# First two units of the Mlp on the attention's list, four weight blocks split in place, another list and another order of evictions

## Chip, cores and metric

The kernel runs on one core of one Trainium2 chip. The metric is the device time of one execution in microseconds, the median of several runs.

## What is computed

The kernel computes a delta-rule attention over 32 heads, then a first Mlp with a rational function between its two products, then a second one with mish.

```python
k_n = k / (np.linalg.norm(k, axis=-1, keepdims=True) + 1e-06)
for t in range(S):                     # q, k, v: (4, 8, 768, 48)
    y[:, :, t] = np.einsum('bhd,bhde->bhe', q[:, :, t], state)
    v_old = np.einsum('bhde,bhd->bhe', state, kt)
    state = state + bt[:, :, :, None] * np.einsum('bhd,bhe->bhde', kt, vt - v_old)
...
h = x @ w_in                           # x: (3072, 384), w_in: (384, 2048)
P = a[0] + a[1] * h + a[2] * h2 + a[3] * h3
Q = 1.0 + np.abs(b[0]) * np.abs(h) + np.abs(b[1]) * h2
x = (P / (Q + 1e-06)) @ w_out          # w_out: (2048, 384)
...
h = x @ w_in                           # the second Mlp, weights of its own
g = h * np.tanh(np.where(h > 20.0, h, np.log1p(np.exp(np.minimum(h, 20.0)))))
out = g @ w_out
```

The weights arrive as float64 and are turned into float32 on the chip.

## The kernel before

**Attention.** The 768 positions are twelve units u of 64, each holding 32 heads. `prepare` loads k and q of a unit, scales k by its norm (`kn`), transposes k and q on TensorE (PE) into `kq`, multiplies them (`gram`, L417) and writes the masked products on VectorE (DVE) into `gm` and `lg` (L426). For every pair of units `inverse` solves a triangular system in 30 steps of two operations (L501, L507), between an opening transpose on DVE (`first`, L489) that needs the masks of both units, and a closing one (`last`, L514) that gives `xt`. For u = 1 and 9 these steps run on DVE, for u = 3, 5, 7 and 11 on GpSimd (POOL). `step` then takes the units one after the other through the state: PE products with S (L561), with xt (L578), with gm (L593), the new state (L601), and y (L616), with small DVE and ScalarE (ACT) operations between them. Step u needs the state that step u-1 left and xt of its pair; xt of u=11 (`xt_152`) serves steps 10 and 11.

**Weights.** `Weights.convert` handles one side (w_in or w_out) of one f block of 128 of the 2048 columns: load the raw block, ACT takes the magnitude (`mag`, L717), DVE makes the float32 word in four operations in the PSUM bank `word` (L722 to L738), ACT writes the high part (`out`, L745) and POOL the rest (`rest`, L750). With high and low parts three matmuls stand for one exact product. Blocks 0 and 1 (`FQ`) stay in SBUF; blocks 2 to 15 are stored to memory and fetched again by the Mlp part.

**The list.** `Plan` holds each operation of the attention, of the first Mlp's weights and of x of the first group, with an engine, a guessed duration, what it reads and what it writes. `order` walks a model of the engines and takes, of what is ready, the operation with the longest tail, shifted by a bias out of the table `ORDER` (by engine, tile name and twelfth of the list). The cost formulas, `Clock` and `ORDER` thus decide the fixed order in which every engine runs. Where the model sees PE idle, matmuls of zeros (L1099) are put in.

**Mlp.** Each Mlp has 96 units: six groups of 512 tokens times sixteen f blocks. A unit is an "up" (nine 128x512 matmuls into one of two PSUM banks h, L870), elementwise work, and a "down" (L956, nine 128x512 matmuls into three of four banks o, or L989 in the second Mlp, twelve 128x384). `MLP_OPS` lists for one iteration, as two-letter operations, what is issued in which order; `LAGS` puts the down four units behind the up. For the first Mlp 1a to 1c are three ACT operations out of h (L900 to L909), 1d a POOL product (L913), 1e and 1f Ln and Exp on ACT (L920, L922) into one of two PSUM banks r, 1g and 1h two DVE operations that read h (L927, L929) and free its bank, 1i to 1k three DVE operations (L936 to L945) that give g; then g is split into a high part (L881) and a low part (L885). At the end of a group y0, y1 and y2 are the copies of the three o banks to SBUF (ACT, L1078); the next group's first down waits for them. In the first iterations only ups are there, so units 0 to 4 go up ahead of the first down. Five fetched blocks (`LOOK`) are asked for at the start of this part.

```python
"fx fw y0 1e 1f y1 u0 u1 u2 1a 1b 1c 1i 1j 1k 1d 1g 1h y2 d0 d1 d2 d3 xa 1L 1m xB f c",
w1.plan(plan, [*range(FQ, NF), *range(FQ)])
fetch_w = {n: (w1.fetch_split, FQ + LOOK + n) for n in range(NF - FQ - LOOK)}
```

Of the kernel before, what the change touches and what calls it, by code (L numbers as in the profile page):

```python
# [43 lines left out]
class Ring:  # L44
# [27 lines left out]
    'ACT s_ps': {-1: -732309, 0: 55802},  # L72
    'ACT w': {-1: 9850, 9: 213571, 10: -105072, 11: 10115},
    'ACT wm': {-1: -117229, 9: -1472, 10: 21445, 11: -42477},
    'ACT x': {-1: 910575, 11: 50160},
    'ACT yst': {-1: 297892, 2: 1553, 3: -60918, 4: 1728, 5: 12465, 6: 156789, 7: -104482, 8: -41027, 9: 6271},
# [30 lines left out]
class Clock:  # L107


    STEP, DOWN, UP, SMALL = 3413.0, 0.57, 0.85, 0.45  # L110

    def __init__(self):
        self.used = {i: self.STEP for i in range(-1, 4)}
        self.at, self.rate = 0, 1.0
# [1107 lines left out]
```

## Time and profile before

| what | us |
|---|---|
| median of three runs | 1132.39 |
| lowest and highest | 1126.92, 1140.34 |
| the profiled execution | 1140.86 |
| its span | 1138.4 |
| PE busy in the span | 1068.5 (94%) |
| first product h of the first Mlp | 322.19 |

The profile is one execution, recorded on the chip. "Busy" is the time in which an engine runs instructions; PE's granted clock is given as a share of its full speed. Idle time is put down to what came last. An "up" of unit i is written u*i*, a "down" d*i* where a list of matmuls is meant.

### The profile page before, as it was taken

The page shows a single profiled execution, that of the slowest core. Times are in us where ns is not written, and L with a number is a line of the kernel's source. Part 1 is how long each engine was busy: PE and PEld are TensorE (multiplying, and loading weights), DVE is VectorE, ACT ScalarE, POOL GpSimd, SP SyncE. Part 2 cuts the span into 40 slices and gives each one's busy share as a digit, 9 for nine tenths or more (in the row PEclk, how much of TensorE's full clock was granted, in tenths as well). Part 3 has the DMA queues.
Part 4 walks back from the last instruction along what each step waited for, and adds up shares of the span by engine and source line. Part 5 has one row for each costly group of instructions (what it writes and reads, how often), then busy time and mean ns, then how long its engine had stood idle before and what let it go on. Part 6 is the DMA issues. An engine that isn't in the chain of part 4 may idle for free.

```text
span 1138.4 us, 24584 instructions
## 1 busy us (share of the span) xinstructions
PE 1068.5 (94%) x10130; PEld 930.9 (82%) x10130; DVE 718.4 (63%) x1207; ACT 612.9 (54%) x1101; POOL 538.9 (47%) x622
## 2 busy tenths in 40 slices
PE   6787889788989999999999999999999999999998
PEld 6677778678867778788787878899999999999997
DVE  4987585896558999999999999994121111212110
ACT  4524445323458888888888888743333223333322
POOL 4187698675436777777777777764000000000000
PEclk8988698977799999999999999999999999999999
DMA  7437686415466031121203026160101001010000
GB/s 127 87 80 187 189 207 185 124 45 157 140 246 241 15 111 43 42 83 43 84 28 112 14 91 254 58 195 14 56 1 56 1 1 56 1 56 1 29 1 28
DMA packets 121263, 99.20 MB, mean 87 GB/s; under 512 B 79808, under 2 KB 104512, under 8 KB 121152
## 3 DMA queue, kind: packets, MB, share of 16 engines
q1 hardware_dynamic: 120896, 97.54, 28.5%
q8 instruction: 79, 1.29, 0.5%
q14 instruction: 32, 0.26, 0.1%
q0 software_dynamic: 256, 0.10, 0.1%
HBM read 66.16 MB, written 31.46 MB: 86 GB/s over the span
## 4 chain that ended last, share of the span: by engine, by line
PE 51%; POOL 15%; ACT 12%; DVE 10%; issue 7%; DMA 2%; SPq 2%; POOLq 0%; DVEq 0%; ACTq 0%
PE h L870 20%; PE o L989 18%; POOL q L913 8%; POOL gh L885 3%; POOL r L903 3%; ACT r L920 3%; PE y_ps L616 3%; PE o L956 3%; PE c_ps L578 2%; ACT q L900 2%; ACT r L922 2%; DVE tmp L501 2%; SPq L291 1%; PE s_all L601 1%; DVE gm L426 1%
## 5 line engine op out<-in xcount | busy, mean ns | idle before, releaser
L870 PE MATMUL h<-x,w 128*128 128x512 f32 x1728 | 430.2, 393 | 5.7 <-DMA w<-w 3.5
L870 PEld LDWEIGHTS h<-x,w 128*128 128x128 f32 x1728 | 322.2, 188 | 75.1 <-DVE s L929 7.2
L885 DVE TENSOR_TENSOR gh<-g,gh 128x512 fp32r<-128x512 f32 x80 | 55.4, 692 | 282.7 <-ACT g L980 282.7
L956 PE MATMUL o<-gh,w 128*128 128x512 f32 x864 | 213.4, 390 | 4.9 <-ACT ev L1078 4.9
L989 PE MATMUL o<-w,gh 128*128 128x384 f32 x1152 | 216.8, 337 | 0.0
L989 PEld LDWEIGHTS o<-w,gh 128*128 128x128 f32 x1152 | 204.6, 188 | 8.1
L956 PEld LDWEIGHTS o<-gh,w 128*128 128x128 f32 x864 | 161.6, 188 | 41.1 <-ACT ev L1078 7.8
L975 ACT ACTIVATE gh<-h 128x512 fp32r<-128x512 f32 x96 | 57.5, 599 | 235.8 <-PE h L870 235.7
L913 POOL TENSOR_TENSOR q<-q,r 128x512 f32<-128x512 f32 x96 | 124.5, 1297 | 71.1 <-ACT r L907 66.6
L885 POOL TENSOR_TENSOR gh<-g,gh 128x512 fp32r<-128x512 f32 x112 | 145.4, 1299 | 23.9 <-ACT g L980 21.4
L920 ACT ACTIVATE r<-q,cst 128x512 f32<-128x512 f32 x96 | 66.4, 692 | 52.6 <-POOL q L913 52.6
L936 DVE SCALAR_TENSOR_TENSOR q<-q,r 128x512 f32<-128x512 f32 x96 | 65.2, 679 | 15.1 <-ACT r L922 14.8
L909 ACT ACTIVATE s<-h,ab 128x512 f32<-128x512 f32 x96 | 74.3, 774 | 0.0
L929 DVE SCALAR_TENSOR_TENSOR s<-s,ab,h 128x512 f32<-128x512 f32 x96 | 71.8, 748 | 3.4
L750 POOL TENSOR_TENSOR w<-wm,w 128x384 fp32r<-128x384 f32 x48 | 49.8, 1040 | 48.6 <-ACT w L745 48.4
L940 DVE SCALAR_TENSOR_TENSOR r<-s,ab,r 128x512 f32<-128x512 f32 x96 | 71.6, 746 | 0.0
L927 DVE TENSOR_TENSOR s<-s,h 128x512 f32<-128x512 f32 x96 | 65.3, 681 | 9.5 <-ACT s L909 9.5
L945 DVE SCALAR_TENSOR_TENSOR g<-q,r 128x512 f32<-128x512 f32 x96 | 65.9, 687 | 3.3
L507 POOL TENSOR_TENSOR xs<-xs,tmp 128x30 f32<-128x30 f32 (+14 forms) x120 | 62.4, 520 | 9.4
L501 POOL TENSOR_TENSOR tmp<-xs 128x30 f32<-128x30 f32 (+14 forms) x120 | 59.4, 495 | 7.1
L881 ACT CAST gh<-g 128x512 fp32r<-128x512 f32 x96 | 59.7, 622 | 0.0
L903 POOL TENSOR_SCALAR r<-q,ab 128x512 f32<-128x512 f32 x54 | 42.1, 780 | 34.8 <-ACT q L900 34.8
(125 smaller groups left out, 1396.9 us busy)
## 6 DMA issues: line engine op xcount, KB each, us to landing
w<-w SPq DMA_DIRECT2D x36, 768.0 KB, 7.1
w<-in_moe_w_in_dram SPq DMA_DIRECT2D x32, 384.0 KB, 3.9
...
```

What stands on the lines that cost most here:

```text
L501: eng.tensor_tensor(out=tv, in0=ls[:, j, j + 1:HC].unsqueeze(1).to_broadcast([128, j, n]), in1=xs[:, 0:j, j:j + 1].to_broadcast([128, j, n ...
L870: self.nc.tensor.matmul(out=self.st[i]["h"], lhsT=self.w.t[f][:, a, 0, k], rhs=self.x[g][:, b, k], start=(n == 0), stop=(n == 8),)
L885: (nc.gpsimd if engine == "P" else nc.vector).tensor_tensor(out=s["gh"][:, 1], in0=s["g"], in1=s["gh"][:, 0].bitcast(F32), op=ALU.subtract)
L903: nc.gpsimd.tensor_scalar(out=s["r"], in0=s["q"], scalar1=k["b1"], scalar2=k["b0"], op0=ALU.mult, op1=ALU.add)
L909: nc.scalar.activation(out=s["s"], in_=s["h"], func=ACTF.Identity, scale=k["a3"], bias=k["a2"])
L913: nc.gpsimd.tensor_tensor(out=s["q"], in0=s["q"], in1=s["r"], op=ALU.mult)
L920: nc.scalar.activation(out=s["r"], in_=s["q"], func=ACTF.Ln, bias=k["c"])
L929: nc.vector.scalar_tensor_tensor(out=s["s"], in0=s["s"], scalar=k["a1"], in1=s["h"], op0=ALU.add, op1=ALU.mult)
L940: nc.vector.scalar_tensor_tensor(out=s["r"], in0=s["s"], scalar=k["a0"], in1=s["r"], op0=ALU.add, op1=ALU.mult)
L945: nc.vector.scalar_tensor_tensor(out=s["g"], in0=s["q"], scalar=2.0, in1=s["r"], op0=ALU.subtract, op1=ALU.mult, reverse0=True)
L956: self.nc.tensor.matmul(out=self.acc[g][d], lhsT=self.w.t[f][:, a, 1, d], rhs=self.st[i]["gh"][:, b], start=(first and n == 0), stop=(last ...
L989: self.nc.tensor.matmul(out=self.acc[g][t][:, 0:384], lhsT=self.st[i]["gh"][:, a, t * 128:(t + 1) * 128], rhs=self.w.t[f][:, b, 1].rearran ...
```

## The change

Six things are changed together.

- Four tiles `wg` of the size of a split weight block are allocated in the outer pool. While the attention runs they hold `gm` 0 to 3; once a gm is dead, one of the blocks 2 to 5 (`FG`) is split into it in place and stays there. Blocks 6 to 15 come first in the list and are the only ones that are stored and fetched again.
- Two tiles `gh` hold the attention's `qn`, and later the split g of units 0 and 1 (`FIRST`).
- The front of units 0 and 1 (up, elementwise work, split of g) joins the attention's list (`Mlp1.plan`). The up goes into the attention's banks `t_ps`; q, s, r and g lie in the buffers of kn 0 to 3, r in SBUF instead of a PSUM bank. The Mlp part leaves these steps out and runs the downs of units 0 and 1 in iterations 2 and 3.
- In the first Mlp's list the second eviction y1 follows y0, ahead of 1e and 1f.
- The model of the list gets another cost for a DVE step of the inverse, other clock thresholds and shares.
- `ORDER` gets other numbers throughout.

```diff
@@ -22,6 +22,8 @@
 FQ = 2
+FG = 4
+FIRST = 2
 LOOK = 5
...
 MLP_OPS = [
-    "fx fw y0 1e 1f y1 u0 u1 u2 1a 1b 1c 1i 1j 1k 1d 1g 1h y2 d0 d1 d2 d3 xa 1L 1m xB f c",
+    "fx fw y0 y1 1e 1f u0 u1 u2 1a 1b 1c 1i 1j 1k 1d 1g 1h y2 d0 d1 d2 d3 xa 1L 1m xB f c",
...
 ORDER = {
...
-    'PE t': {-1: -21846, 0: -41437, 1: -19183, 2: -111019, 3: 2549, 4: 77091, 5: -6842, 6: 33694, 7: 33160},
+    'PE t': {-1: -579786, 0: -3742057, 1: 1883379, 2: 6418149, 3: 1342676, 4: -214248, 5: 2760576, 6: 1072462, 7: -2081211, 11: -2132370},
...
@@ -244,10 +262,11 @@
-        self.qn = ring("qn", self.NQ, [128, M, DP])
+        self.qn = [t.rearrange("p a t -> p (a t)").rearrange("p (m d) -> p m d", m=M) for t in hosts["gh"]]
...
-        self.gm = ring("gm", self.NT, [128, M, HC + C])
+        self.gm = [t.rearrange("p a b k c -> p (a b k c)").rearrange("p (m d) -> p m d", m=M) for t in hosts["wg"]]
+        self.gm += ring("gm", self.NT - len(self.gm), [128, M, HC + C])
...
-            cost = 3.9 * n + 560 if engine == "POOL" else 2.1 * n + 300 if early else 2.8 * n + 240
+            cost = 3.9 * n + 560 if engine == "POOL" else 2.1 * n + 300 if early else 0.5 * n + 1000
...
@@ -757,9 +779,10 @@
-        slots = len(self.kept)
         for i, f in enumerate(fs):
-            slot, late = f"w{i % slots}", LATE * i - AHEAD
+            slot, late = [f"w{i % FQ}"], LATE * i - AHEAD
+            if f in self.kept and f >= FQ:
+                slot = [f"gm{f - FQ}{j}" for j in range(4)]
...
@@ -916,7 +940,8 @@
         if 0 in parts:
-            s["r"] = self.ps.tile([128, TOK], F32, "r")
+            if "g" not in s:
+                s["r"] = self.ps.tile([128, TOK], F32, "r")
...
+    def plan(self, p, i, f, h, hb, rooms):
+
+        (a, ab), (b, bb) = rooms
+        self.st[i] = {"h": h, "q": a[:, 0], "s": a[:, 1], "r": b[:, 0], "g": b[:, 1]}
+        ups = self.up(i, 0, f)
+        n = {x: f"m{x}{i}" for x in ("q", "s", "r", "g", "gh")}
+        p.add("PE", 2050, lambda: [fn() for fn in ups], ["x0", "x1", "x2", f"w{f}"], [hb])
+        p.add("ACT", 600, lambda: self.e1(i, [0]), [hb], [n["q"], ab])
+        p.add("ACT", 760, lambda: self.e1(i, [2]), [hb, ab], [n["s"]])
+        p.add("POOL", 780, lambda: self.e1(i, [1]), [n["q"]], [n["r"], bb])
+        p.add("POOL", 1280, lambda: self.e2(i), [n["r"]], [n["q"]])
+        p.add("DVE", 690, lambda: self.e4(i, [0]), [hb], [n["s"]])
+        p.add("DVE", 750, lambda: self.e4(i, [1]), [hb], [n["s"]])
+        p.add("ACT", 690, lambda: self.e3(i, [0]), [n["q"]], [n["r"]])
+        p.add("ACT", 590, lambda: self.e3(i, [1]), (), [n["r"]])
+        p.add("DVE", 690, lambda: self.e5(i, [0]), [n["r"]], [n["q"]])
+        p.add("DVE", 750, lambda: self.e5(i, [1]), [n["s"]], [n["r"]])
+        p.add("DVE", 690, lambda: self.e5(i, [2]), [n["q"], n["r"], bb], [n["g"]])
+        p.add("ACT", 620, lambda: self.hi(i, "A"), [n["g"]], [f"qn{i}", n["gh"]])
+        p.add("POOL", 1300, lambda: self.lo(i, "P"), [n["g"]], [n["gh"]])
...
-    sb.add(sb1, w=FQ, w64=2, wm=2, x=1, xraw=1)
+    sb.add(sb1, w=FQ, wg=FG, gh=FIRST, w64=2, wm=2, x=1, xraw=1)
...
-    w1 = Weights(nc, moe_w_in, moe_w_out, sb, range(FQ), (), wd[0])
+    w1 = Weights(nc, moe_w_in, moe_w_out, sb, range(FQ + FG), (), wd[0])
...
-        w1.plan(plan, [*range(FQ, NF), *range(FQ)])
+        w1.plan(plan, [*range(FQ + FG, NF), *range(FQ + FG)])
...
+        m1.pool = range(FIRST)
+        for i in range(FIRST):
+            rooms = [
+                (at.kn[2 * i + j].rearrange("p m d -> p (m d)").rearrange("p (a t) -> p a t", a=2), f"kn{2 * i + j}")
+                for j in range(2)
+            ]
+            m1.plan(plan, i, i, at.t_ps[i], f"t{i}", rooms)
...
-        sb.add(sb2, w=16 - FQ, wt=1, w64=1, wm=1, x=1, q=3, s=3, r=2, g=3, gh=5, ev=3)
+        sb.add(sb2, w=NF - FQ - FG, wt=1, w64=1, wm=1, x=1, q=3, s=3, r=2, g=3, gh=5 - FIRST, ev=3)
...
-                    if 0 <= j < n2 and mlp(j) is m:
+                    if FIRST <= j < n2 and mlp(j) is m:
...
-                elif op[0] == "u" and i < n2:
+                elif op[0] == "u" and FIRST <= i < n2:
...
+                elif op[0] == "d" and 0 <= i - FIRST < FIRST:
+                    if i - FIRST not in downs:
+                        downs[i - FIRST] = down(i - FIRST)
+                    n = int(op[1])
+                    run(downs[i - FIRST][0][3 * n:3 * n + 3])
```

What the new list does to the engines is seen in three places. The first is PE, from the last steps of the attention to the first downs. Before, the last rows of steps 10 and 11 (y and c banks) and then the Mlp part:

```order
L616 MATMUL y_ps_172<-gm_142,u_145 48x64 x16
L578 MATMUL c_ps_168<-r_146,xt_152 32x48 x16
L616 MATMUL y_ps_172<-kq_136,su_144 48x64 x16
L616 MATMUL y_ps_172<-gm_142,u_145 48x64 x16
L870 MATMUL h<-x,w 128x512 x45
L956 MATMUL o<-gh,w 128x512 x9
L870 MATMUL h<-x,w 128x512 x9
L956 MATMUL o<-gh,w 128x512 x9
```

After, on PE: the two ups stand within step 10.

```order
L612 MATMUL c_ps_169<-u_145,gm_141 32x48 x16
L612 MATMUL c_ps_168<-u_145,gm_141 32x48 x16
L893 MATMUL t_ps_170<-x,w 128x512 x9
L597 MATMUL c_ps_169<-r_146,xt_152 32x48 x16
L597 MATMUL c_ps_168<-r_146,xt_152 32x48 x16
L893 MATMUL t_ps_171<-x,w 128x512 x9
L620 MATMUL s_all_167<-u_145,kn_132 48x48 x32
```

The Mlp part on PE then begins in this way after the change, with the last y of step 11 ahead of it.

```order
L635 MATMUL y_ps_172<-gm_142,u_145 48x64 x16
L893 MATMUL h<-x,wg 128x512 x9
L1002 MATMUL o<-gh,w 128x512 x9
L893 MATMUL h<-x,wg 128x512 x9
L1002 MATMUL o<-gh,w 128x512 x9
L893 MATMUL h<-x,wg 128x512 x18
L893 MATMUL h<-x,w 128x512 x9
L1002 MATMUL o<-gh,wg 128x512 x9
```

Five ups in a row have become one up and one down in turn; the blocks of the first ups are those that stayed in `wg`.

The second place is DVE at the end of the inverse of u=1, whose closing transpose gives xt of steps 0 and 1 (`xt_150`). Before:

```order
L501 TENSOR_TENSOR tmp_153<-yst_155,s_all_167 128x58
L507 TENSOR_TENSOR s_all_167<-s_all_167,tmp_153 128x29x2
L501 TENSOR_TENSOR tmp_153<-yst_155,s_all_167 128x30
L507 TENSOR_TENSOR s_all_167<-s_all_167,tmp_153 128x30
L511 TENSOR_TENSOR s_all_167<-s_all_167,beta_121 128x1024
L514 STREAM_TRANSPOSE xt_150<-s_all_167 128x32x32
L529 MEMSET s_all_167 128x1024
```

After, on DVE, the opening transpose for u=5 (`xs_148<-lg_147`) stands ahead of the last step:

```order
L520 TENSOR_TENSOR tmp_153<-yst_155,s_all_167 128x58
L526 TENSOR_TENSOR s_all_167<-s_all_167,tmp_153 128x29x2
L508 STREAM_TRANSPOSE xs_148<-lg_147 128x1024
L520 TENSOR_TENSOR tmp_153<-yst_155,s_all_167 128x30
L526 TENSOR_TENSOR s_all_167<-s_all_167,tmp_153 128x30
L530 TENSOR_TENSOR s_all_167<-s_all_167,beta_127 128x1024
L533 STREAM_TRANSPOSE xt_150<-s_all_167 128x32x32
```

It stood behind the closing transpose before, with the masks of u=5 that it needs. The opening transpose for u=3, on the other hand, comes after 8 of the 30 steps of this inverse instead of 15, so 22 steps lie between it and xt_150 instead of 15.

The third place is the end of DVE's list of the attention. Before, the last weight operations are followed by one subtraction of step 11 and the first Mlp operation that reads h:

```order
L569 TENSOR_TENSOR r_146<-r_146,c_ps_169 128x384
L722 TENSOR_SCALAR word_166<-wm 128x384
L726 TENSOR_SCALAR word_166<-word_166 128x384
L732 SCALAR_TENSOR_TENSOR word_166<-w_4550,word_166 128x384
L738 SCALAR_TENSOR_TENSOR wm<-w_4550,word_166 128x384
L569 TENSOR_TENSOR r_146<-r_146,c_ps_168 128x384
L927 TENSOR_TENSOR s<-s,h 128x512
```

After, on DVE, with both sides of block 5 (`w_4583` and `w_4783` are their raw blocks):

```order
L754 SCALAR_TENSOR_TENSOR word_166<-w_4583,word_166 128x384
L760 SCALAR_TENSOR_TENSOR wm<-w_4583,word_166 128x384
L588 TENSOR_TENSOR r_146<-r_146,c_ps_168 128x384
L744 TENSOR_SCALAR word_166<-wm 128x384
L748 TENSOR_SCALAR word_166<-word_166 128x384
L754 SCALAR_TENSOR_TENSOR word_166<-w_4783,word_166 128x384
L760 SCALAR_TENSOR_TENSOR wm<-w_4783,word_166 128x384
L952 TENSOR_TENSOR s<-s,h 128x512
```

A whole side of weights now stands between the last subtraction and the first h, in the bank `word`, which the first h takes over.

## Rows read from the trace of the kernel before

**Rows 1.** The page's head
```profile
span 1138.4 us, 24584 instructions
```

**Rows 2.** Stretches: from:to us, length, busy us of each engine, PE clock, DMA share, GB/s
```profile
294.30:308.00 13.70, 12.17 (x314) 11.46 (x314) 5.67 (x11) 4.48 (x10) 4.01 (x4) 0.61 0.79 224
308.00:322.20 14.20, 14.11 (x461) 13.21 (x459) 6.43 (x12) 5.59 (x11) 1.99 (x2) 0.90 0.09 20
322.20:1138.40 816.20, 801.02 (x3747) 687.14 (x3744) 489.75 (x736) 479.67 (x840) 342.28 (x294) 1.00 0.19 68
339.07:739.00 399.93, 393.68 (x1715) 319.41 (x1714) 377.96 (x563) 341.20 (x579) 303.27 (x261) 1.00 0.25 89
```

**Rows 3.** PE timeline, start of the Mlp part: start, us, operation, [idle before, releaser]
```profile
322.19 4.40 PE L870 MATMUL h<-x,w 128*128 128x512 f32 x18
330.12 5.92 PE L870 MATMUL h<-x,w 128*128 128x512 f32 x18 [3.54 <-DMA w<-w]
336.89 2.34 PE L870 MATMUL h<-x,w 128*128 128x512 f32 x9 [0.85 <-DVE s L929]
339.07 2.21 PE L956 MATMUL o<-gh,w 128*128 128x512 f32 x9
```

**Rows 4.** PE's waits in 340 to 745: line, waited for, us, times, longest
```profile
PE o L956 <- ACT ev L1078: 4.9, 5, 1.5
```

**Rows 5.** ACT timeline at the first change of group
```profile
406.22 0.59 ACT L1078 COPY ev<-o 128x512 f32<-128x512 f32 x1
407.42 0.69 ACT L920 ACTIVATE r<-q,cst 128x512 f32<-128x512 f32 x1 [0.61 <-POOL q L913]
408.15 0.58 ACT L922 ACTIVATE r<-r 128x512 f32<-128x512 f32 x1
408.64 0.59 ACT L1078 COPY ev<-o 128x512 f32<-128x512 f32 x1
```

**Rows 6.** DVE timeline around the start of the Mlp part
```profile
316.66 0.55 DVE L738 SCALAR_TENSOR_TENSOR wm<-w,word 128x384 int32<-128x384 int32 x1
327.45 0.75 DVE L929 SCALAR_TENSOR_TENSOR s<-s,ab,h 128x512 f32<-128x512 f32 x1
```

**Rows 7.** PE timeline, steps 10 and 11
```profile
297.56 1.49 PE L593 MATMUL c_ps<-u,gm 32*32 32x48 f32 x32 [0.95 <-ACT u L585]
306.66 1.95 PE L561 MATMUL c_ps<-su,kq 64*64 64x48 f32 x32 [0.58 <-ACT su L609]
```

**Rows 8.** Lines of POOL and DVE in 0 to 325: count | busy, mean ns | idle
```profile
L750 POOL TENSOR_TENSOR w<-wm,w 128x384 fp32r<-128x384 f32 x32 | 32.0, 999 | 48.5 <-ACT w L745 48.4
L726 DVE TENSOR_SCALAR word<-word 128x384 int32<-128x384 int32 x32 | 18.1, 566 | 1.1
```

**Rows 9.** POOL's waits in 56 to 222
```profile
POOL w L750 <- ACT w L745: 16.1, 11, 5.3
```

**Rows 10.** DVE timeline in the attention
```profile
54.25 0.42 DVE L507 TENSOR_TENSOR s_all<-s_all,tmp 128x240 f32<-128x240 f32 x1
54.58 1.97 DVE L489 STREAM_TRANSPOSE xs<-xraw 128x1024 f32<-128x1024 f32 x1
66.84 1.01 DVE L426 TENSOR_TENSOR gm<-t_ps,mask 128x384 f32<-128x384 f32 x2
70.81 2.00 DVE L514 STREAM_TRANSPOSE xt<-s_all 128x1024 f32<-128x1024 f32 x1
163.13 2.10 DVE L514 STREAM_TRANSPOSE xt<-xs 128x1024 f32<-128x1024 f32 x1
233.57 2.43 DVE L507 TENSOR_TENSOR xs<-xs,tmp 128x234 f32<-128x234 f32 x1
292.13 2.11 DVE L514 STREAM_TRANSPOSE xt<-xs 128x1024 f32<-128x1024 f32 x1
```

**Rows 11.** POOL timeline, the beginning of the inverse of u=11
```profile
233.33 2.41 POOL L492 TENSOR_TENSOR xs<-xs,beta 128x1024 f32<-128x1024 f32 x1 [13.53 <-DVE xs L489]
```

**Rows 12.** The page's groups of instructions
```profile
L913 POOL TENSOR_TENSOR q<-q,r 128x512 f32<-128x512 f32 x96 | 124.5, 1297 | 71.1 <-ACT r L907 66.6
```

More of the change, by code (lines that the diff above doesn't have):

```diff
@@ L64 @@
 ORDER = {
[7 rows of a table removed]
[L72 to L76, printed above, removed]
[6 rows of a table removed]
-    'DVE s_ps': {-1: 6686, 0: 29, 1: -191256},
-    'DVE wm': {-1: -284625, 9: -82236, 10: 215159, 11: -119412},
-    'DVE word': {-1: -351263, 9: -12057, 10: 117330, 11: 4839},
@@ L104 @@
+    'DVE s_ps': {-1: -3568170, 0: 640246},
+    'DVE wm': {-1: 3821251, 9: -3015317, 10: -1849336, 11: -807657},
+    'DVE word': {-1: -7099687, 9: -2199399, 10: 3089149, 11: 524067},
+    'DVE xs': {-1: -795099, 1: 931567, 2: 2464624, 4: -4207757, 5: -310981, 6: -1764569, 7: 1605068},
+    'DVE xt': {-1: 1611379, 0: -288246, 1: 2419816, 3: 895398, 4: 3402972, 6: 341539, 7: 20157},
+    'DVE yst': {-1: 1072339, 0: -4411530},
[6 rows of a table added]
+    'POOL mgh': {-1: 4849205, 11: -3139120},
[12 rows of a table added]
 }
 class Clock:
-    STEP, DOWN, UP, SMALL = 3413.0, 0.57, 0.85, 0.45
+    STEP, DOWN, UP = 3413.0, 0.508, 0.826
@@ L112, in __init__, with run @@
     def __init__(self):
[L113 to L117 removed]
+        self.used = {i: [self.STEP, self.STEP] for i in range(-1, 3)}
+        self.at, self.rate = -1, 1.0
+    def run(self, t, ns, shares=(1.0, 1.0)):
+        while ns > 1e-3:
             i = int(t // self.STEP)
             while self.at < i:
[L120 to L121 removed]
+                low, high = (x / self.STEP for x in self.used.get(self.at, (0, 0)))
+                self.rate = (0.5 if low < self.DOWN else 1.0) if self.rate == 1.0 else 1.0 if high >= self.UP else 0.5
@@ L124, in run @@
             took = took if took > 0 else 1
-            self.used[i] = self.used.get(i, 0) + took * share
+            used = self.used.setdefault(i, [0, 0])
+            if i >= 3:
+                for n in range(2):
+                    used[n] += took * shares[n]
             ns -= took * self.rate
@@ L194, in order @@
                     zeros[i] = max(0, int((t - last - max(0, self.IDLE - gone)) * 0.9 // self.ZEROS))
-                    last = clock.run(last, zeros[i] * self.ZEROS, 1.0)
+                    last = clock.run(last, zeros[i] * self.ZEROS)
                     if last < t:
@@ L198, in order @@
                     t = max(t, last)
-                small = self.names[i][0] in ("c0", "c1") and self.ops[i][1] == 860
-                end = clock.run(t, self.ops[i][1], clock.SMALL if small else 1.0)
+                name = self.names[i][0]
+                small = name in ("c0", "c1") and self.ops[i][1] == 860
+                end = clock.run(t, self.ops[i][1], (0.5, 0.36) if small else (0.96, 1.06) if name[0] == "s" else (1.0, 1.0))
             else:
@@ L771, in plan @@
                 p.add("DVE", 570, low, [raw, "word"], [m], early=late)
-                p.add("ACT", 500, out, [m], [slot], early=late)
-                p.add("POOL", 1000, rest, [m], [slot], early=late)
+                p.add("ACT", 500, out, [m], slot, early=late)
+                p.add("POOL", 1000, rest, [m], slot, early=late)
             if f not in self.kept:
-                p.add("SP", 2500, lambda f=f: self.store(f), [slot], (), more=2500, early=late)
+                p.add("SP", 2500, lambda f=f: self.store(f), slot, (), more=2500, early=late)
     def store(self, f):
@@ L866, in fn @@
             def fn():
-                if n == 0:
+                if n == 0 and i not in self.st:
                     self.st[i] = {"h": self.ps.tile([128, TOK], F32, "h")}
```

36 lines of the change are left out of this document (21 added, 15 removed), and 65 rows, old and new, of the table ORDER.

## The prediction

> **What bounds the kernel now.** I read the page's head first: it gives the span [rows 1]. The profiled execution took 1140.9 us, 2.5 more than that span, and 8.5 more than the median of the three runs, 1132.4. I make the sum against 1140.9 and subtract the result from 1132.4, because nothing in the change depends on what made that one execution longer.
>
> Then I read the stretches [rows 2]. From 322.2, where the first Mlp product starts, to the end at 1138.4 are 816.2 us, and TensorE (PE) is busy in 801.0 of them, at a mean clock of 1.00. So the Mlp part is PE's own work, and only 15 us of it are gaps. Ahead of 322.2 no engine is full. There the attention's chain counts: inverses on POOL and DVE, then two steps for each.
>
> The PE timeline at the start of the Mlp part [rows 3] shows most of those gaps. Nine 128x512 matmuls, one product "up", last 4.40 / 2 = 2.2 us at this place and some 2.08 in the long run (393.68 us for 1715 recorded matmuls of 128x512, nine a product, give 2.07). Five ups stand ahead of the first product "down" at 339.07, so 16.9 us pass for 10.4 us of work: 3.54 us idle for a weight block on its way back from memory, 18 matmuls in 5.92 at a lower clock, 0.85 behind a VectorE (DVE) operation. The start costs 6.5 us.
>
> The waits of the first Mlp [rows 4] hold one regular gap: PE waits for an eviction of the o banks, 5 times, 4.9 us in all, once at each change of the token group. ScalarE's (ACT) timeline shows why [rows 5]: the eviction at 408.64 stands behind the Ln and Exp of a unit, and ACT had idled 0.61 us before that Ln.
>
> **The change part by part, and its cost.**
>
> *Units 0 and 1 leave the Mlp part.* Two ups of 2.08 are gone from PE's full stretch: **-4.2**.
>
> *The start.* The list becomes u2 d0 u3 d1 u4 u5 u6 d2. An up must find an h bank free, which its DVE operation frees: h0 is ready at 322.19 + 2.20 = 324.39 and the s operation ends at 327.45 + 0.75 = 328.20 [rows 3, 6], 3.8 us later. With 2.08 for each product u4's matmuls end at 10.4, u6 needs that bank at 12.5, and it is free at 14.2: 1.7 us idle. The other ups find theirs free. Blocks 2 to 5 are in SBUF, so no up before u6 needs a fetch; 12.5 us is later than the 7.9 us that the first fetch needs now (330.12 - 322.19). So 6.5 becomes 1.7 to 2: **-4.5**. If fetches still come late, 3.5 of it is lost.
>
> *The second eviction ahead of Ln and Exp.* It can follow the first one, about 1.2 us earlier than 408.64. PE's wait goes from 4.9 to nearly nothing; the unit's Ln comes 0.6 later, and ACT's idle 0.61 covers that. **-4.5** (0 to -4.9). Without that cover Ln would be 0.6 late, five times 0.6 = 3 us at most. The change from the first to the second Mlp runs by the other list and stays as it is.
>
> *The two ups inside the last steps.* xt(11) is done at 292.13 + 2.11 [rows 10] and PE needs 294.30 to 322.20, 27.9 us, for steps 10 and 11. It is busy in 12.17 of 13.70 us and 14.11 of 14.20, with a clock of 0.61 and 0.90 [rows 2]. Two ups add 4.2 at the full clock and 8.3 at half. Of the gaps, 0.95 and 0.58 [rows 7] can be filled, 1.5. I take the full clock, since dense 128x512 work is what ran at 0.90 to 1.00: **+2.7** (0 to +8.3). Their 26 elementwise operations run on ACT, POOL and DVE below. DVE is busy 5.67 + 6.43 = 12.1 us of these 27.9; ten operations of the fronts (7 us) and eight more of the weights (4.5) still fit.
>
> *DVE's end.* The first h of the Mlp part takes the bank that held `word`. Before, the last operation on it ran at 316.66 [rows 6], 5 us early. After, it is the last DVE row ahead of the first operation on h, and its raw block is loaded only when the raw buffer of the side before is free. Four operations of 0.56 [rows 8], 2.3 us, may stand behind PE's last step. **+1** (0 to +3).
>
> *The list of the attention.* This is the widest unknown. On POOL the chain from the inverse of u=3 to that of u=7 holds weight operations ("rest"): I count 22 in the list before, 17 after. One costs 1.0 [rows 8] and a mean wait for ACT's half of 16.1 / 22 = 0.73 [rows 9]; five fewer give -8.7. On DVE 88 operations of the weights precede the start of the inverse of u=9, and 80 after: 8 x 0.56 = -4.5. Both lead to the last steps, so I take the middle, **-6**. The bounds: with all of POOL's waits for ACT gone too, -5.0 - 16.1 = -21. Above: between the transpose that starts the inverse of u=3 (54.58) and xt(1) (70.81), DVE now has seven more steps of two operations of up to 0.42, eight more masks (two gm of 1.01 a pair, so with the smaller lg about 3), and a transpose of 2 [rows 10]: 5.9 + 2.9 + 1.9 = +10.7 for xt(1).
>
> *A port.* At 233.57 a DVE operation on two SBUF operands took 2.43 us, while POOL's 233.33 operation ran to 235.74 [rows 10, 11]. A similar one at 54.25, with an operand in PSUM, took 0.42. The units 0 and 1 now keep r in SBUF, so their six last DVE operations have two SBUF operands. Each could lose the length of a POOL operation, 1.3 [rows 12]: 0 to +7.8. I take nothing, since g of unit 0 is needed only behind step 11 and u2, some 25 us on.
> The Trainium skill (SBUF — State Buffer, "Who interferes with whom") says that a DVE instruction with two SBUF inputs contends with a GpSimd instruction that reads SBUF, and that the loser waits for the whole instruction. The trace agrees: 2.43 against 0.42 us. By that rule alone all six could be caught, and the sum would be 7.8 higher.
>
> Sum: -4.2 - 4.5 - 4.5 + 2.7 + 1 - 6 = **-15.5**, so 1125.4 for an execution like the profiled one and **1117** against the median.
>
> **The rivals.**
>
> *R1, only the Mlp part gains.* The list gives nothing (0 for -6), and the ups run at half clock (+8.3 for +2.7). For it: the clock at 294 to 308 is 0.61, and the chain up there wanders over all engines. Against it: POOL's and DVE's shorter counts. -15.5 + 6 + 5.6 = -3.9: 1128.5.
>
> *R2, POOL was the whole limit.* The list gives its bound, -21 for -6: -30.5, 1102. For it: 16.1 us of waits on one engine that runs three inverses in a row. Against it: fewer operations take away their own waits, not those of the other 17.
>
> *R3, slower: xt(1) arrives 10.7 us later and all of it reaches the end.* The place is DVE between 54.6 and 72.8, where the inverse of u=1 now gives way to the preparation of later units. +10.7 for -6: -15.5 + 16.7 = +1.2, 1133.6. It ends above the old time once more than 9.5 of the 10.7 come through. Against it: from xt(1)'s end at 72.81 to xt(5) at 163.13 four steps run in 90 us [rows 10], where two need 27.9 at the end, four some 56. So 34 us are slack there, if the inverses start in time.
>
> *R4, the port.* The six operations are caught, and DVE's work for step 11 and g of units 0 and 1 fall behind: +7.8, 1124.7. Against it: the order is loose there.
>
> **How the numbers follow.** My forecast has a chance of 0.50, R1 0.16, R2 0.12, R3 0.12, R4 0.10. The likeliest gives 1117. Its own range comes from its three large unknown terms, start, evictions and list, which may together be 8 us off either way: 1109 to 1125. The range 1102 to 1134 reaches to R2 below and to R3 above; beyond them lie about half of R2, half of R3 and a late end of R1, some 2 in 10. About 1% is what a measurement of this kernel can tell from no change: faster is below 1121.1, slower above 1143.7. Of the forecast some three quarters lie below 1121 (0.38), nearly all of R2 (0.11), and of R1 and R4 about a third (0.08): 0.57. Slower needs R3 together with the ups at half clock (1133.6 + 5.6) or with late fetches: half of it, 0.06. The rest, 0.37, is no change.
>
> **What would show it.** Right: the first up of the Mlp part starts near 320 (322.2 + 2.7 + 1 - 6), and the first seven ups and downs wait under 2.5 us in all; PE's wait for evictions in the first Mlp is below 1 us; the two ups in the last steps take 2.1 to 2.7 each. The list is right if xt(5) comes some 3 us ahead of 163.13 and xt(11) some 6 ahead of 292.13. Wrong: an idle PE of 2 us or more before its first h (DVE's end), a wait for fetches before u6, xt(5) or xt(11) no earlier than before. If xt(11) is late by more than 9 us, everything won in the Mlp part is gone.

## The result, and the profile after

The changed kernel takes **1125.95 us** in the median of 20 runs, the kernel before 1135.44 in the median of 20. That is 9.5 us less, where 15.5 were forecast. The ratio is 0.9899, with a 95% interval of 0.988 to 0.9918; it goes by the means, without the changed kernel's longest run (1134.31 us, counted as slow), while the medians alone give 0.992. The time lies inside the range of 1102 to 1134. The 1% that the prediction set for "faster" lies inside the interval, so these runs do not decide whether it was passed.

The two profiled executions are 14.4 us apart (1140.86 and 1126.43), more than the medians. The first one misleads, as the experiments show.

PE's timeline of the changed kernel at the end of the attention and at the start of the Mlp part; the columns are start, length, operation, and the idle time before it with its releaser:

```profile
294.37 2.33 PE L893 MATMUL t_ps<-x,w 128*128 128x512 f32 x9
298.11 2.35 PE L893 MATMUL t_ps<-x,w 128*128 128x512 f32 x9
...
319.36 2.35 PE L893 MATMUL h<-x,wg 128*128 128x512 f32 x9 [1.56 <-DVE wm L760]
321.55 2.21 PE L1002 MATMUL o<-gh,w 128*128 128x512 f32 x9
323.59 2.20 PE L893 MATMUL h<-x,wg 128*128 128x512 f32 x9
325.63 2.20 PE L1002 MATMUL o<-gh,w 128*128 128x512 f32 x9
327.67 4.24 PE L893 MATMUL h<-x,wg 128*128 128x512 f32 x18
333.64 2.37 PE L893 MATMUL h<-x,w 128*128 128x512 f32 x9 [1.72 <-DVE s L954]
```

Against [rows 3], the wait for a fetched block (3.54 us) and the slow stretch of 5.92 us are gone. What is left is 1.72 us ahead of the up of unit 6. The two ups in step 10 take 2.33 and 2.35 us, so they run at full clock. New is the wait of 1.56 us ahead of the first h, for DVE's last weight operation in the bank `word`.

The waits of PE in the first Mlp, from 340 to 745 (line, waited for, us, times, longest), have one row. In the kernel before there was, beside the row of [rows 4], one for the same operation on DVE:

```profile
PE h L893 <- DVE s L954: 3.1, 8, 0.6
```

```profile
PE h L870 <- DVE s L929: 1.2, 4, 0.4
```

The wait for evictions of [rows 4] is gone. ACT at the first change of group shows why, with the two copies in one row ahead of the Ln; PE shows what came in its place:

```profile
394.64 1.08 ACT L1124 COPY ev<-o 128x512 f32<-128x512 f32 x2
395.81 0.69 ACT L945 ACTIVATE r<-q,cst 128x512 f32<-128x512 f32 x1
```

```profile
397.18 2.35 PE L893 MATMUL h<-x,wg 128*128 128x512 f32 x9 [0.24 <-DVE s L954]
```

The Mlp part, in the view of stretches (length, then busy us of PE, PEld, DVE, ACT and POOL, PE's clock, DMA share, GB/s):

```profile
319.36:1124.70 805.34, 795.38 (x3726) 682.79 (x3726) 482.15 (x726) 473.10 (x829) 337.10 (x290) 1.00 0.19 65
```

Against [rows 2] it is 10.9 us shorter, 5.6 in PE's work and 5.2 in gaps. The attention ahead of it ends only 2.8 us earlier (319.36 for 322.19). DVE's closing transposes give xt(1), xt(3), xt(5), xt(9) and xt(11); below them are xt(3) and xt(9) of the kernel before, which [rows 10] does not have:

```profile
81.82 1.92 DVE L533 STREAM_TRANSPOSE xt<-s_all 128x1024 f32<-128x1024 f32 x1
104.06 2.08 DVE L533 STREAM_TRANSPOSE xt<-xs 128x1024 f32<-128x1024 f32 x1 [0.29 <-POOL xs L530]
159.38 2.10 DVE L533 STREAM_TRANSPOSE xt<-xs 128x1024 f32<-128x1024 f32 x1
...
249.76 2.08 DVE L533 STREAM_TRANSPOSE xt<-xs 128x1024 f32<-128x1024 f32 x1
286.92 2.12 DVE L533 STREAM_TRANSPOSE xt<-xs 128x1024 f32<-128x1024 f32 x1
```

```profile
102.58 2.09 DVE L514 STREAM_TRANSPOSE xt<-xs 128x1024 f32<-128x1024 f32 x1
...
259.55 2.08 DVE L514 STREAM_TRANSPOSE xt<-xs 128x1024 f32<-128x1024 f32 x1
```

xt(1) comes 11.0 us later than in [rows 10] (10.7 were worked out), but xt(3) only 1.5 later, and xt(5) is 3.8 earlier, xt(9) 9.8 and xt(11) 5.2. So each sign that the prediction named for "right" is met by this profile, those of the list (some 3 and 6 us) too. The experiments correct that.

### The profile page after: what moved, and what is told of

It reads as the page before. It is cut to its first block, busy times and chain, and to the rows that moved or that the text cites. A ratio compares the mean times of both kernels' runs of the same rounds, so it can differ in the third digit from the quotient of the medians.

```text
span 1124.7 us, 24637 instructions
## 1 busy us (share of the span) xinstructions
PE 1060.0 (94%) x10172; PEld 920.8 (82%) x10172; DVE 720.8 (64%) x1207; ACT 610.8 (54%) x1100; POOL 541.2 (48%) x623
## 3 DMA queue, kind: packets, MB, share of 16 engines
q8 instruction: 79, 1.29, 0.5%
## 4 chain that ended last, share of the span: by engine, by line
PE 50%; POOL 15%; DVE 12%; ACT 12%; issue 7%; DMA 3%; SPq 2%; POOLq 0%; DVEq 0%; ACTq 0%
PE h L893 20%; PE o L1035 18%; POOL q L937 7%; POOL gh L908 3%; PE o L1002 3%; ACT r L945 3%; POOL r L927 3%; PE c_ps L597 2%; ACT q L924 2%; ACT r L947 2%; PE y_ps L635 2%; DVE tmp L520 1%; SPq L310 1%; PE c_ps L580 1%; PE s_all L620 1%
## 5 line engine op out<-in xcount | busy, mean ns | idle before, releaser
L893 PE MATMUL h<-x,w 128*128 128x512 f32 x1278 | 318.0, 393 | 3.9 <-DVE s L954 3.6
L893 PEld LDWEIGHTS h<-x,w 128*128 128x128 f32 x1278 | 237.0, 188 | 56.5 <-DVE s L954 10.2
L1035 PE MATMUL o<-w,gh 128*128 128x384 f32 x864 | 162.5, 337 | 0.0
L1002 PE MATMUL o<-gh,w 128*128 128x512 f32 x648 | 159.2, 390 | 0.0
L1035 PEld LDWEIGHTS o<-w,gh 128*128 128x128 f32 x864 | 153.4, 188 | 6.0
L908 POOL TENSOR_TENSOR gh<-g,gh 128x512 fp32r<-128x512 f32 x110 | 142.6, 1297 | 23.8 <-ACT g L1026 21.4
L937 POOL TENSOR_TENSOR q<-q,r 128x512 f32<-128x512 f32 x94 | 122.0, 1297 | 61.6 <-ACT r L931 57.2
L1002 PEld LDWEIGHTS o<-gh,w 128*128 128x128 f32 x648 | 121.5, 188 | 26.0 <-ACT ev L1124 0.8
L893 PE MATMUL h<-x,wg 128*128 128x512 f32 x432 | 107.0, 392 | 2.8 <-DVE wm L760 1.6
L893 PEld LDWEIGHTS h<-x,wg 128*128 128x128 f32 x432 | 80.5, 188 | 19.9 <-DVE s L954 2.5
```

The source lines that it names most:

```text
L893: self.nc.tensor.matmul(out=self.st[i]["h"], lhsT=self.w.t[f][:, a, 0, k], rhs=self.x[g][:, b, k], start=(n == 0), stop=(n == 8),)
L908: (nc.gpsimd if engine == "P" else nc.vector).tensor_tensor(out=s["gh"][:, 1], in0=s["g"], in1=s["gh"][:, 0].bitcast(F32), op=ALU.subtract)
L937: nc.gpsimd.tensor_tensor(out=s["q"], in0=s["q"], in1=s["r"], op=ALU.mult)
L1002: self.nc.tensor.matmul(out=self.acc[g][d], lhsT=self.w.t[f][:, a, 1, d], rhs=self.st[i]["gh"][:, b], start=(first and n == 0), stop=(last ...
L1035: self.nc.tensor.matmul(out=self.acc[g][t][:, 0:384], lhsT=self.st[i]["gh"][:, a, t * 128:(t + 1) * 128], rhs=self.w.t[f][:, b, 1].rearran ...
```

## The experiments

**The kernel before, once more.** No edit.

> The unchanged kernel before, profiled a second time. Question: the profiled execution of before took 1140.9 us, that of the change about 1127, but the medians are 1135.4 and 1126.0. Theory A: the profile of before was a long one of a kernel whose runs spread by 16 us, and its excess over the median (5.4 us) lies where transfers are waited for: ahead of 322.2 or in the 3.54 us wait for the first fetched block. Then this profile is shorter, near 1133 to 1137, and differs from the first one in these places and not behind 340. Theory B: the excess is spread over the Mlp part. Then the stretch from the first h to the end is not 816 us but 811 or less.

It took 1130.74 us, less than the 1133 to 1137 expected. The first h stands at 311.89, 10.3 us earlier than in the first profile. The rows are PE's first ups, xt(9) and xt(11) on DVE, and the Mlp part:

```profile
311.89 4.39 PE L870 MATMUL h<-x,w 128*128 128x512 f32 x18
319.76 5.97 PE L870 MATMUL h<-x,w 128*128 128x512 f32 x18 [3.48 <-DMA w<-w]
```

```profile
251.77 2.07 DVE L514 STREAM_TRANSPOSE xt<-xs 128x1024 f32<-128x1024 f32 x1
281.39 2.12 DVE L514 STREAM_TRANSPOSE xt<-xs 128x1024 f32<-128x1024 f32 x1
```

```profile
311.89:1128.20 816.31, 800.97 (x3748) 687.19 (x3744) 489.67 (x736) 479.70 (x840) 342.41 (x294) 1.00 0.19 68
```

The Mlp part lasts 816.31 us here and 816.20 in the first profile. What differs is the attention. xt(11) came at 281.39, not at 292.13 [rows 10], with the same list. Theory A holds in its main point: the scatter lies ahead of the first h, not behind it. But it does not lie in the wait for the fetch (3.48 for 3.54), where I had placed a part of it. The forecast measured the new list against an attention that was slow that once. A third execution of the same list follows from the next run.

**The evictions alone**, in the kernel before:

```diff
-    "fx fw y0 1e 1f y1 u0 u1 u2 1a 1b 1c 1i 1j 1k 1d 1g 1h y2 d0 d1 d2 d3 xa 1L 1m xB f c",
+    "fx fw y0 y1 1e 1f u0 u1 u2 1a 1b 1c 1i 1j 1k 1d 1g 1h y2 d0 d1 d2 d3 xa 1L 1m xB f c",
```

> The kernel before with the second eviction ahead of Ln and Exp and nothing else. Theory of the prediction: the 4.9 us of waits for evictions go and nothing comes back, -4.5 us (ratio 0.996). Rival, after the trace of the change: the Ln comes later, its unit's ACT and DVE operations on h too, and the next up waits for DVE instead; about 2 us come back, so -3 us (ratio 0.9975), with PE's waits for the eviction near 0 and its waits for the DVE operation on h at 3 us in place of 1.2.

1133.86 us against 1135.8; ratio 0.9973, interval 0.9943 to 1.0003, so the time alone does not tell it from no gain. PE's timeline at the start and its waits in 318 to 745:

```profile
324.18 4.40 PE L870 MATMUL h<-x,w 128*128 128x512 f32 x18
```

```profile
PE h L870 <- DVE s L929: 3.9, 9, 0.8
PE h L870 <- DMA w<-w: 3.3, 1, 3.3
```

Without the 0.82 of the start, PE waits 3.1 us for DVE in 8 places and never for an eviction, as in the changed kernel; before, it was 4.9 and 1.2. So the profile gives 3.0 of the 4.9 us as won, as the rival said. The first h came at 324.18: three executions of one list of the attention gave 322.2, 311.9 and 324.2.

**The two units back in the Mlp part**, the list otherwise in its new order. In `Mlp1.plan` each function becomes empty, and the Mlp part's bounds start at 0 again:

```diff
-        p.add("ACT", 600, lambda: self.e1(i, [0]), [hb], [n["q"], ab])
+        p.add("ACT", 600, lambda: None, [hb], [n["q"], ab])
...
-                elif op[0] == "u" and FIRST <= i < n2:
+                elif op[0] == "u" and i < n2:
```

> The change, but the up and the elementwise work of units 0 and 1 are taken out of the attention's list (the order of all else is kept) and stand in the Mlp part as before; the blocks 2 to 5 stay in SBUF. It tells the two units apart from the kept blocks and the list. Theory: two ups cost 4.2 in the Mlp part, and its start has five ups ahead of the first down again, with waits for DVE of some 3 us instead of 1.7, but no wait for a fetch; in the attention's last steps 1 to 3 us are won back. So 2.5 to 5 us slower than the change, ratio to before 0.992 to 0.9945. Rival: the gain is all in the kept blocks and the list, and the ups in the last steps cost as much as they save: ratio 0.990.

1133.09 us; ratio 0.9976, interval 0.9949 to 1.0002. By the medians that is 7 us slower than the change, more than I had expected. PE's waits from 310 to 740:

```profile
PE h L893 <- DVE s L954: 8.4, 12, 1.7
PE h L893 <- DVE wm L760: 1.6, 1, 1.6
```

Three ups at the start wait 1.67 to 1.75 each for their bank, 5.2 in all, where the change has one such wait. The Mlp part, 1128.3 - 314.8 = 813.5 us, is 8.1 longer than with the two units on the list (4.2 for two ups, 3.4 for two more waits). No row is left for a fetched block, so the kept blocks do take that wait away; the waits for banks stand in its place. So most of the change's gain is these two units. Without them the kept blocks and the list are worth little. The other way round, the two units without the kept blocks, was not run.

**The old numbers of the list**, with all else changed:

```diff
-    STEP, DOWN, UP = 3413.0, 0.508, 0.826
+    STEP, DOWN, UP, SMALL = 3413.0, 0.57, 0.85, 0.45
...
-            cost = 3.9 * n + 560 if engine == "POOL" else 2.1 * n + 300 if early else 0.5 * n + 1000
+            cost = 3.9 * n + 560 if engine == "POOL" else 2.1 * n + 300 if early else 2.8 * n + 240
```

and `ORDER` as before, without entries for the operations that the change adds.

> The change with the numbers of ORDER, the clock model and the cost of a DVE step as before; the two units on the list, the kept blocks and the evictions stay. Theory: the new numbers are what brings xt(11) from 292.1 to 286.9 and the order of weights that fits to it. Without them the list loses that, 5 us or more, and the biases do not fit the changed list, so it could lose more: ratio to before 0.995 to 1.01, with xt(11) at 292 or later. Rival: the kept blocks alone shorten POOL's list, since fewer weights must come before the gm are dead; then xt(11) is near 287 here too and the ratio is 0.990.

1145.84 us; ratio 1.0065, interval 1.0028 to 1.0102. By the medians it is 20 us slower than the change, and it is slower than the kernel before. Its xt(9) and xt(11), in a profile that was shorter than its median:

```profile
267.93 1.96 DVE L517 STREAM_TRANSPOSE xt<-xs 128x1024 f32<-128x1024 f32 x1
299.60 2.10 DVE L517 STREAM_TRANSPOSE xt<-xs 128x1024 f32<-128x1024 f32 x1
```

The table belongs to its list of operations, and the longer list needs new numbers. The rival (xt(11) near 287 from the kept blocks alone) is out under these numbers. What the new order is worth against the old one is another question, for which the zeros below are needed.

**Another bank for the first h.** The o banks are allocated first, so d0 and not the first up takes over the weights' bank:

```diff
-                if first and j == 0:
+                if first and j == 0 and g not in self.acc:
...
         ps.add(ps2, h=2, o=4, r=2)
+        m1.acc[0] = [ps.tile([128, TOK], F32, "o") for _ in range(3)]
```

> The change with one edit: the o banks are allocated ahead of the h banks, so that the bank which held the weights' word becomes an o bank, first written by d0, one up later. Theory: PE's wait of 1.56 us before its first h (for DVE's last weight operation) goes, since d0 comes 2 us behind; 1 to 1.6 us faster than the change, ratio to before 0.9885. Rival: the weight operations are late by themselves, and what they release (block 5's second side, or another attention bank that h now takes over) holds PE as long; no gain, and the wait has another name.

1125.28 us; ratio 0.9889, interval 0.9848 to 0.993. The wait is gone:

```profile
319.16 2.33 PE L893 MATMUL h<-x,wg 128*128 128x512 f32 x9
```

PE has no other wait there, so the theory is right on the mechanism; a gain of 1.6 us is too small for the times to show against the attention's scatter.

**In addition, the down of unit 2 ahead of the up of unit 6:**

```diff
-            for op in LISTS[kind]:
+            ops = LISTS[kind]
+            if i == 6:
+                ops = [x for x in ops if x not in ("d0", "d1", "d2")]
+                at = ops.index("u0")
+                ops = ops[:at] + ["d0", "d1", "d2"] + ops[at:]
+            for op in ops:
```

> The edit of the run before, and the down of unit 2 moved ahead of the up of unit 6. Theory: the up of unit 6 waited 1.72 us for the DVE operation on h of unit 4; with a down of 2.1 us in between it finds the bank free; another 1.2 to 1.7 us faster, ratio to before 0.987. Rival: g of unit 2 is not ready 12.5 us behind its up's start, and PE waits there for as long for POOL's low part: no gain.

1123.18 us; ratio 0.988, interval 0.9838 to 0.9922. PE's timeline:

```profile
329.25 2.39 PE L1002 MATMUL o<-gh,wg 128*128 128x512 f32 x9 [0.63 <-ACT gh L904]
...
334.34 2.33 PE L893 MATMUL h<-x,w 128*128 128x512 f32 x9 [0.66 <-DVE s L954]
```

Instead of 1.72 us there are 0.63 for the split of g (its high part, on ACT) and 0.66 for the next bank, 1.29 together. The Mlp part is no shorter for it: 1121.5 - 316.0 = 805.5 us from the first h to the end, as with the o banks alone (1124.6 - 319.2 = 805.4). So the rival is right, and the 2 us between the two medians are scatter of the attention.

**Ten us more DVE work ahead of xt(1), and ahead of xt(9)** (the second with `u == 9`):

```diff
         def last():
+            if u == 1:
+                for _ in range(5):
+                    nc.vector.transpose(out=xt.rearrange("p n t -> p t n"), in_=xs.rearrange("p j i -> p i j"))
```

> The change with 10 us more work on DVE right ahead of xt(1): its closing transpose is run six times instead of once, with the same result. The rival R3 of the prediction said that a later xt(1) runs through to the end. Theory: some 34 us are slack between xt(1) and xt(5) in before, 11 of them were used up by the change; 10 more still fit mostly: +0 to +4 us, xt(5) late by less than 4. R3: +8 to +10 us.

> The same 10 us of DVE work ahead of xt(9). Theory: behind xt(9) the steps 8 to 11 follow without slack, so 8 to 10 us reach the end, and xt(9) is what the list must bring forward. Rival: in the change xt(9) is done at 251.8 and xt(11) at 289.0, 37 us for two steps that need some 28 to 30, so 5 to 9 us of the delay are absorbed ahead of xt(11), and the end moves by 1 to 5 us.

Ahead of xt(1): 1133.77 us, ratio 0.9962, interval 0.9925 to 0.9999, 8 us above the change by the medians. The theory fell; what R3 feared is possible. xt(1) ended 11 us later, and so did xt(3):

```profile
92.90 1.89 DVE L536 STREAM_TRANSPOSE xt<-s_all 128x1024 f32<-128x1024 f32 x1
115.11 2.00 DVE L536 STREAM_TRANSPOSE xt<-xs 128x1024 f32<-128x1024 f32 x1
```

POOL's row for one weight operation, here and then in the change:

```profile
98.78 0.99 POOL L775 TENSOR_TENSOR w<-wm,w 128x384 fp32r<-128x384 f32 x1 [10.81 <-ACT w L770]
```

```profile
87.73 1.00 POOL L772 TENSOR_TENSOR w<-wm,w 128x384 fp32r<-128x384 f32 x1 [1.09 <-ACT w L767]
```

The POOL row shows the way. In the middle of the inverse of u=3 POOL's list has a weight operation. It needs ACT's half of that block; ACT's stands behind two copies of step 0, which need xt(1), and needs DVE's, which stands behind xt(1) too. The inverse, which needs nothing of it, stops for 10.8 us. In the change itself the same operation cost it 1.09 us. The slack of 34 us that the prediction read off the distance of xt(1) and xt(5) was slack in the chain of states, not in the engines' lists.

Ahead of xt(9): 1134.65 us, ratio 0.997, interval 0.9939 to 1.0, 8.7 us above the change by the medians:

```profile
296.35 2.14 DVE L536 STREAM_TRANSPOSE xt<-xs 128x1024 f32<-128x1024 f32 x1
```

Here the theory is right. xt(9) came 10.0 us later and xt(11) 9.4, so next to nothing was absorbed between them.

**Zeros in steps 8 and 9.** In the change PE waits three times between xt(9) and step 9, and the clock falls:

```profile
251.90 1.55 PE L597 MATMUL c_ps<-r,xt 32*32 32x48 f32 x64 [0.62 <-DVE xt L533]
253.35 1.55 PE L612 MATMUL c_ps<-u,wg 32*32 32x48 f32 x64
256.21 1.72 PE L597 MATMUL c_ps<-r,xt 32*32 32x48 f32 x64 [1.31 <-DVE r L588]
257.86 2.52 PE L620 MATMUL s_all<-u,kn 64*48 64x48 f32 x64
261.71 3.27 PE L580 MATMUL c_ps<-su,kq 64*64 64x48 f32 x64 [1.33 <-ACT su L628]
```

The same 64 small products last 1.55 at 251.90 and 1.72 at 256.21. In narrower stretches the clock is 0.86 in 256 to 258, 0.50 from 258 to 286 and 0.73 in 286 to 290. In wider ones (columns as above):

```profile
260.00:280.00 20.00, 17.99 (x366) 16.62 (x364) 9.17 (x18) 6.38 (x14) 15.29 (x27) 0.50 0.34 90
280.00:300.00 20.00, 20.00 (x497) 18.43 (x496) 11.42 (x18) 8.25 (x17) 8.89 (x9) 0.80 0.49 122
```

A clock of 0.50 is the lower of the two levels, 1.2 GHz. PE is busy in nearly all of this stretch, and xt(9) to xt(11) takes 37.2 us, 29.6 in the second profile of before. How PE holds up xt(11), a DVE operation on POOL's result, is seen in two rows of the change:

```profile
277.26 1.91 POOL L530 TENSOR_TENSOR xs<-xs,beta 128x1024 f32<-128x1024 f32 x1
```

```profile
286.44 0.55 DVE L588 TENSOR_TENSOR r<-v,c_ps 128x384 f32<-128x384 f32 x1 [4.82 <-PE c_ps L580]
```

POOL is done with the inverse of u=11 at 279.17. But in DVE's list the closing transpose (286.92) stands right behind a subtraction of step 10, and that waits 4.82 us for a PE product. The edit puts zeros into PE's gaps (ten matmuls in the first kernel, 4, 6 and 8 in the second):

```diff
+        def hot(n, f):
+            return lambda: ([self.heat(True) for _ in range(n)], f())
...
-                p.add("PE", 900, ks(h), [f"{kqb}00", f"{kqb}01", s], [c])
+                p.add("PE", 900, hot(4 if u == 9 and h else 0, ks(h)), [f"{kqb}00", f"{kqb}01", s], [c])
...
-            p.add("PE", 860, uu(h, 0), [r if u else vb, xb], [c])
+            p.add("PE", 860, hot(2 if u == 8 and h else 0, uu(h, 0)), [r if u else vb, xb], [c])
...
-            p.add("PE", 860, uu(h, 1), [r, xb, "y_ps"] if h else [r, xb], [c])
+            p.add("PE", 860, hot(4 if u == 8 and h else 0, uu(h, 1)), [r, xb, "y_ps"] if h else [r, xb], [c])
```

> The change with ten matmuls of zeros more on PE in the first part of steps 8 and 9: two ahead of the first product with xt of step 8, four ahead of its second, four ahead of the first product with the state of step 9, where PE idled 0.62, 1.31 and 1.33 us at full clock in the change. Theory: the clock of 0.50 that ran from 258 to 287 in the change is what swallowed the list's gain of 9.8 us at xt(9), since PE was busy 18 to 20 of 20 us there; with the gaps filled the clock stays up, steps 8 and 9 shorten to some 29 us from 37, and the Mlp part starts 5 to 9 us earlier: ratio to before 0.982 to 0.986. Rival: the clock falls all the same, or the steps wait for POOL's inverse of u=11 (its last operation ended at 279 in the change) and DVE; then the start moves by less than 2 us, ratio 0.989 to 0.990.

> The same with 4, 6 and 8 matmuls of zeros. Theory: if the clock falls with ten it may stay up with eighteen, at a cost of up to 2.5 us for zeros that are longer than the gaps; the start of the Mlp part 3 to 7 us earlier than in the change, ratio 0.983 to 0.987. If ten are enough, it is 1 to 3 us slower than ten. Rival: as above, no earlier start; then 1 to 2.5 us slower than the change.

With ten zeros 1123.05 us (ratio 0.9891, interval 0.9853 to 0.993), with eighteen 1121.92 (0.9885, 0.9836 to 0.9934). The stretch, with ten:

```profile
260.00:280.00 20.00, 15.65 (x523) 14.33 (x523) 10.31 (x20) 7.86 (x17) 16.27 (x31) 1.00 0.47 127
280.00:300.00 20.00, 18.14 (x550) 16.04 (x546) 13.54 (x24) 10.41 (x21) 11.20 (x11) 1.00 0.47 123
```

The clock stays at 1.00 (with eighteen it is 0.91 and 1.00), and xt(9) to xt(11) takes 30.1 us (30.9). So it is shown that the fallen clock stretched these steps. The gain in time is 3 to 4 us by the medians, 1 to 2 by the ratios, less than the 5 to 9 of the theory and not clear of the intervals. With ten zeros the same subtraction still holds xt(11) (283.60), though for less; POOL's inverse, whose last operation ends at 281.30, does not:

```profile
283.12 0.56 DVE L588 TENSOR_TENSOR r<-v,c_ps 128x384 f32<-128x384 f32 x1 [1.43 <-PE c_ps L580]
```

**All three together** (o banks first, the down of unit 2 early, eighteen zeros).

> The three edits together on the change: the o banks allocated ahead of the h banks, the down of unit 2 ahead of the up of unit 6, and the 4, 6 and 8 matmuls of zeros in steps 8 and 9. Theory: the gains lie in different places and add up: 1.56 for the first h, 1.1 for the up of unit 6, 4 for the clock, so some 5 to 7 us below the change, near 1119 to 1121, ratio to before 0.984 to 0.987. Rival: with the first h no longer held, the last steps end by y and nothing is gained there beyond the zeros; 1121 to 1123, ratio 0.9885.

**1116.50 us** in the median of 6 runs (1113.89 to 1119.55) against 1134.71; ratio 0.9825, interval 0.9786 to 0.9864. The first h comes at 312.28 without a wait:

```profile
312.28 2.35 PE L896 MATMUL h<-x,wg 128*128 128x512 f32 x9
```

The sum of the theory is exceeded: by the medians this is 9.5 us below the change, and the two intervals of the ratio do not meet, so the three edits together are a gain over the change. But they do not add up as the theory had it. From the first h to the end are 1117.8 - 312.3 = 805.5 us, 805.3 in the change, so the down of unit 2 gave nothing, and all of the gain lies ahead of the first h. Why it is more there than the 1.56 us and the 3 to 4 us of the zeros is not shown.

## Why the prediction was right or wrong

The forecast was 15.5 us, 9.5 were measured; 1125.95 us lies in the wide range and 1 us above the forecast's own, 1109 to 1125. Of the 9 us between it and 1117, 3 come from the reference: the median of 20 runs of before is 1135.4, that of the first three was 1132.4.

The Mlp part repeats (816.2 and 816.3 us in two profiles of before, 805.3 to 805.7 in the nine profiles with the two units on the list), so each median gives the typical attention: the median less the Mlp part, less what lies around the span. That is 1135.4 - 2.5 - 816.2 = 316.7 us for before, 1126.0 - 1.7 - 805.3 = 319.0 for the change, and 1133.1 - 1.7 - 813.5 = 317.9 without the two units on the list. The forecast's terms against that:

| term | forecast | measured | from |
|---|---|---|---|
| two ups out of the Mlp part | -4.2 | -4.1 | PE's work is 5.6 less, of it 1.5 the slow ups of [rows 3] |
| the start | -4.5 | -4.2 | gaps 3.54 + 0.85 become 1.72; 5.92 becomes 4.4 |
| evictions | -4.5 | -3.0 | 4.9 + 1.2 become 3.1 |
| two ups in the last steps | +2.7 | +1.1 | 319.0 - 317.9 |
| the weights' bank | +1 | +1.6 | the wait of 1.56 |
| the list of the attention | -6 | -0.4 | 317.9 - 1.6 - 316.7 |
| sum | -15.5 | -9.0 | measured in all: -9.5 |

The rows of the two ups in the last steps and of the list are differences of medians whose intervals are some 3 us wide either way; the others come from profiles. The 0.5 us between the last two figures are 0.8 less around the span (1.7 for 2.5) and 0.4 that the rows of the Mlp part count too much.

- **Wrong: the list.** The step "Both lead to the last steps, so I take the middle" let what POOL and DVE save reach the end in full, and had no term for PE's clock in steps 8 and 9. The profiles by order of the attention, without those with the old numbers or added DVE work:

  | order of the attention | runs | xt(9) | xt(9) to xt(11) | clock in 260 to 280 |
  |---|---|---|---|---|
  | old | before, once more, evictions alone | 259.6, 251.8, 256.8 | 32.6, 29.6, 30.6 | 0.83, 1.00, 1.00 |
  | new | change, units back, other bank, down early | 249.8, 247.8, 252.8, 250.0 | 37.2, 36.6, 35.0, 36.0 | 0.50, 0.50, 0.59, 0.50 |
  | new, with zeros | ten, eighteen, all three | 253.5, 251.3, 252.9 | 30.1, 30.9, 29.3 | 1.00, 0.91, 1.00 |

  On the mean the new order has xt(9) 5.9 us earlier than the old one, about what was forecast, but xt(11) only 0.7: steps 8 and 9 ran at half clock and gave the rest back. With zeros xt(11) is 4.3 earlier. These are few profiles, and the columns of xt(9) overlap; that the gain ahead of xt(9) comes from POOL's five and DVE's eight operations less is not shown either. And the reference was bad: the attention of before ends at 312 to 324 with one and the same list, and the profile that the terms were read from was one of the long ones. So it is luck that xt(11) came 5.2 earlier than there: its 286.9 is about the mean of the three profiles of the old order, 287.0. That I subtracted the sum from the median was right only for terms that do not depend on what made that execution slow; the text said that none did, and the list did.
- **Mis-sized: the evictions.** The prediction looked for what comes back at the Ln, and there nothing came back: it starts 1.20 us behind the first copy's start before (407.42 for 406.22 in [rows 5]) and 1.17 after (395.81 for 394.64). What it left out is the next up's wait for its h bank. The DVE operation that frees it ended at 408.73 before, while PE waited for the eviction until 409.29; at 397.13 after, when PE waited for nothing else. In all, the waits for DVE rise from 1.2 to 3.1. Three of the eight lie at a change of group; how the order brings the other five is not shown.
- **Right: the start**, with its only wait at u6 (1.7 forecast, 1.72 measured) and no fetch that is late; **the ups** at full clock; **the bank**, with its place and size (1.56 in the range of 0 to 3).
- **R3** had the right price (xt(1) 11.0 later, 10.7 worked out) and did not come true. The inverse of u=3 runs on POOL and began at 57.41 for 56.63 before; the weight operations in it, through which a late xt(1) could hold it, waited 1.3 us in all, so xt(1) to xt(3) shrank from 31.8 (102.58 - 70.81) to 22.2 us. My reason against R3, the slack, was wrong, as 10 us of additional work at that place showed: 8 came through.
- **R4**, the port: two of the six operations began while POOL worked, and these two are the longer ones. One took 0.80 us at 302.49 for 0.68 of its like at 306.79; the other stands here with its like, on DVE:

```profile
304.59 1.34 DVE L965 SCALAR_TENSOR_TENSOR kn<-kn,ab,kn 128x512 f32<-128x512 f32 x1
...
307.99 0.74 DVE L965 SCALAR_TENSOR_TENSOR kn<-kn,ab,kn 128x512 f32<-128x512 f32 x1
```

  POOL worked from 301.99 to 305.39, with next to no pause, and stood still until 308.80. The 0.6 us are off the path. The Trainium skill's rule (SBUF — State Buffer, "Who interferes with whom") agrees with these rows. The other four were not tested by it, since POOL stood still when they began.
- **R2** did not come: the list gave nothing near its 21 us. That POOL is off the path does not follow: with 10 us more DVE work ahead of xt(1), POOL stopped for 10.8 us and 8 us reached the end.
- **R1** is nearest to what happened in its terms (list near 0, Mlp part alone), but without its half-clock ups. R4's 1124.7 lies nearest to the measured time, by chance.

What stays open: why executions of one list part by 10 us and more. The clocks differ (0.67 and 0.93 between 120 and 140 in the two profiles of before), and a stretch at half clock can delay what the next one is made of; what tips the first of them was not tried. Nor is it shown which gaps lower the clock: the zeros show that it stays up when these are filled, but in the same run PE waited 2.19 us ahead of 279.34, and the clock stayed at 1.00.
